# Left keys' values of four heads in one 64x32-tile pass behind a score burst, and g_q*g_k as a per-partition scale in the copy of transposed queries

## The chip, the cores and the metric

The kernel runs on one core of a Trainium2 chip. The metric is the device time in microseconds of one execution; where a kernel was run several times, the median is given.

## The reference

Two parts follow each other. Attention with normalised queries and keys, 8 batches, 12 heads, 448 positions, head dimension 64:

```
q_n = q / sqrt(mean(q*q) + 1e-6) * g_q          # the same for k with g_k
scores = q_n @ k_n.T / sqrt(64)
attn = softmax(scores)
x = attn @ v                                     # heads side by side: 3584 x 768
```

and a multiplicative feed-forward part on the 3584 x 768 result:

```
h = ((x @ w1) * (x @ w2)) @ w3                   # 768 -> 1024, 1024 -> 1024
out = h @ w_out                                  # 3584 x 768, float32
```

## The kernel before

**Quads and units.** Four heads of one batch are a "quad"; there are 24, three per batch. A quad's 448 keys are three full blocks of 128 (`NF` = 3) and 64 left keys (`REST`). Left keys of heads 0 and 1 lie in partitions 0 to 63 of the fourth value block, those of heads 2 and 3 in partitions 64 to 127; the other half of that block is zero or belongs to the other pair. The scores are made transposed, keys on partitions, in seven "units" a quad: `qk_exp` (L464) takes two PSUM banks, runs eight matmuls on 64x32 tiles (two heads on the two row tiles, four column tiles), and ScalarE takes the exponential of both banks into `P`, or into `Pr` for the left keys (L478). Units are issued in "bursts" of three (`G`).

**Sums and values.** `pv_set` (L494) is called three times a quad. Kind 0 multiplies `P` by ones: the softmax sums, of which ScalarE makes the reciprocal `r` as exp(-ln(sum)) (L507, L509). Kinds 1 and 2 multiply by the lower and the upper 32 columns of each head's values. Each is a set of four passes (`j` = 0 to 3) of four matmuls on 128x32 tiles, one head to a column tile, in one bank; the fourth pass is for the left keys. VectorE multiplies the bank by `r` into `xT` (L517). The places of the three kinds are set by `KIND`: steps of one unit behind the quad's last burst.

**Feed-forward fillers.** `ffn1_a` makes `a_sb` = x @ w1, `ffn1_b` multiplies x @ w2 by it into `abT` (L596), `ffn2` multiplies `abT` by `w34s` = w3 @ w_out into `o_sb`; all three go through `narrow` (L530), 24 or 32 matmuls on 128x32 tiles in one bank. These wait in a list, and the loop at the end puts some of them behind each unit's step (`UNITS`, `V_COST`), so that TensorE has work while ScalarE makes exponentials. At the start, while weights are still landing, w3 is transposed (`w3_transpose`, L546) and multiplied by w_out (`w34_unit`, L558).

**Preparation.** For each quad and each pair of heads: squares on ScalarE (L342), their sums on VectorE (L351), the factor `alpha` on ScalarE, and three multiplications on VectorE (`prep_scale`): queries by alpha (L383), that by g_q*g_k from `g_b`, which holds the product in every partition (L390), and keys by alpha (L397). For the first five quads (`N_PE_T`) TensorE transposes queries and keys (`prep_pe_transpose`, L432), with one VectorE copy of both from one bank (two banks and two copies in quad 0); for the rest a DMA on SP's queue does (L409).

**Who sets the order.** The program is written out by hand: a planner keeps an estimated clock of TensorE, ScalarE and VectorE (`clk`), the time at which each of the eight banks becomes free (`free`; `take` gives the earliest) and the landing times of the loads (`LAND`). From these it decides at the time of writing where each preparation and each eviction stands in its engine's stream (`drain`, `evac`; `SLACK`, `PACE`, `URGE`, `LATE` are its margins). `evac` chooses between ScalarE and VectorE where a string such as `A_EV = 'AD'` allows both. Nothing of this is decided while the kernel runs: each engine works through its stream in order and waits for semaphores. Weights and values are loaded on POOL's queue in the order of `LOADS`, queries and keys of later quads on SP's.

Of the kernel before, what the change touches and what calls it, by code (L numbers as in the profile page):

```python
# [18 lines left out]
def kernel(  # L19
# [32 lines left out]
    O_BUFS = 3  # L52
    F_BUFS = 9
    G = 3
    KIND = (2, 3, 6)
    N_PE_T = 5
    N_SQ_ACT = 24
    A_EV = 'AD'
    O_EV = 'AD'
    W_EV = 'DA'  # L60
    BIAS = 0.6
    SLACK = (0.5, 0.2)
    EXP_SLACK = 1.05
    WARM = 16
    WARM_GAP = 0.3
    PACE = 1.1
    SLACK_0 = (2.4, 0.6)
    URGE = 0.3
    AHEAD = 0.0
    LAG = 7  # L70
    UNITS = 1.45
    V_COST = 0.75
    V_AHEAD = 11
    LOAD_AT = -23
    LATE = 6
    T0 = 8.0
    LOADS = ['w1', 'q1', 'w0', 'o0', 'w2', 'v0', 'q2', 'w3', 'w4', 'w5', 'w6', 'v1', 'w7', 'o1', 'v2', 'x0', 'x1', 'v3']
    GATE = None
    GATE_T = {1: 13.0, 2: 11.0}
    AVAIL = 15.0  # L80
    LAND = {'g': 5.6, 'q1': 10.4, 'w0': 11.6, 'w1': 12.9, 'o0': 18.4, 'w2': 20.1, 'v0': 23.8, 'q2': 27.0, 'w3': 28.6, 'w4': 30.3, 'w5': 32.0, 'w6': 33.6, 'v1': 37.2, 'w7': 38.5, 'o1': 45.2, 'v2': 48.1, 'x0': 56.0, 'v3': 61.3, 'x1': 64.5, 'q3': 23.9, 'q4': 37.0, 'q5': 52.5, 'q6': 69.6}

    const = ctx.enter_context(tc.tile_pool(name="const", bufs=1))
    load_pool = ctx.enter_context(tc.tile_pool(name="load", bufs=3))
# [114 lines left out]

    ENG = {"A": "ACT", "D": "DVE"}  # L200

    def copy(e, out, in_):
        if e == "ACT":
            nc.scalar.copy(out=out, in_=in_)  # L204
        else:
            nc.vector.tensor_copy(out=out, in_=in_)  # L206

    def copy_out(z, out, in_, engs, n, bf=False):
        c = {"A": 0.19 + 0.81e-3 * n, "D": 0.12 + (0.55e-3 if bf else 1.06e-3) * n}
        return evac(  # L210
            z, clk["PE"], [ENG[x] for x in engs], [c[x] for x in engs],
            lambda e: copy(e, out, in_),
        )

    w1s = const.tile([128, CM, DFF], BF, name="w1s")
# [3 lines left out]
    w3s = big_pool.tile([128, CF, DFF], BF, tag="big", name="w3s")  # L219
    w3T = big_pool.tile([128, CF, DFF], BF, tag="big", name="w3T")  # L220
    g_row = const.tile([1, 2, D], FP, name="g_row")
    gp_row = const.tile([1, D], BF, name="gp_row")
    ones_row = const.tile([1, NP], BF, name="ones_row")
    g_b = const.tile([NP, D], BF, name="g_b")
    ident = const.tile([128, 128], BF, name="ident")
    ones = const.tile([NP, 3, HALF], BF, name="ones")
    warm_t = const.tile([128, 512], BF, name="warm_t")
# [65 lines left out]
    def load_w12(z):  # L293
        dst, src = ((w1s, moe_w1), (w2s, moe_w2))[z]
        for h in range(HQ):
            for half in range(2):
                nc.gpsimd.dma_start(
                    out=dst[h * HALF : (h + 1) * HALF, half::2, :],
                    in_=src.rearrange(
                        "(s h a d) f -> h a d s f", s=NQB, h=HQ, a=2, d=HALF  # L300
                    )[h, half],
                )
# [68 lines left out]
    def prep_scale(i, pr, part):  # L371
        s = st[i]
        hs = slice(2 * pr, 2 * pr + 2)
        alpha = s["alpha"]
        if "qkT" not in s:
            s["qkT"] = qkT_pool.tile([128, 2, 2, J * NP], BF, tag="qkT", name="qkT")
        if ("qks", pr) not in s:
            live["qks"] += 1
            s["qks", pr] = prep_pool.tile([NP, 2, J, 2, D], BF, tag="qks", name="qks")
        n = rows_of(i, 0)  # L380
        if part == 0:
            s["qtmp"] = prep_pool.tile([NP, J, 2, D], BF, tag="qtmp", name="qtmp")
            nc.vector.tensor_tensor(  # L383
                out=s["qtmp"][0:n].transpose([0, 2, 1, 3]),
                in0=s["q"][0:n, hs],
                in1=alpha[0:n, 0, hs].unsqueeze(3).broadcast_to([n, 2, J, D]),
                op=MULT,
            )
        elif part == 1:
            nc.vector.tensor_tensor(  # L390
                out=s["qks", pr][0:n, 0],
                in0=s["qtmp"][0:n],
                in1=g_b[0:n].unsqueeze(1).unsqueeze(1).broadcast_to([n, J, 2, D]),
                op=MULT,
            )
        else:
            nc.vector.tensor_tensor(  # L397
                out=s["qks", pr][:, 1].transpose([0, 2, 1, 3]),
                in0=s["k"][:, hs],
                in1=alpha[:, 1, hs].unsqueeze(3).broadcast_to([NP, 2, J, D]),  # L400
                op=MULT,
            )
# [11 lines left out]
    def prep_pe_transpose(i, pr):  # L414
# [1 line left out]
        issued.add(("t", i, pr))  # L416
        live["qks"] -= 1
        qks = s.pop(("qks", pr))
        both = i == 0
        if not both:  # L420
            ps, z = take(1)
            ps = ps.bitcast(BF)[:, 0 : 2 * S].rearrange("p (t s) -> p t s", t=2)
        for t in (1, 0) if i == 0 else (0, 1):
            if both:
                ps, z = take(1)
                dst = ps.bitcast(BF)[:, 0:S]
            else:
                dst = ps[:, t]
            w = NP0 if rows_of(i, t) < NP else NP
            for j in range(J):  # L430
                n = min(w, S - j * w)
                nc.tensor.transpose(  # L432
                    dst[:, j * w : j * w + n], qks[0:n, t, j], ident[0:n, 0:n]
                )
            run("PE", 0.25)
            if both:
                s["t_at", pr] = copy_out(
                    z, s["qkT"][:, pr, t, 0:S], dst, "DA"[t] if pr == 0 else "D", S, True
                )
        if not both:  # L440
            s["t_at", pr] = copy_out(z, s["qkT"][:, pr, :, 0:S], ps, "D", 2 * S, True)

# [34 lines left out]
        ))  # L479


    def pv_set(i, kind):
        s = st[i]
        b, m = divmod(i, NQB)
        flush_exps()
        ps, z = take(1)
        ps = ps[:, 0:S]
        for j in range(J):
            for h in range(HQ):
                if kind:  # L490
                    w = s["v"][:, h, j, (kind - 1) * HALF : kind * HALF]
                else:
                    w = ones[:, 0 if j < NF else 1 + h // 2, :]
                nc.tensor.matmul(  # L494
                    out=ps[h * HALF : (h + 1) * HALF, :],
                    lhsT=w,
                    rhs=s["P"][:, h, j, :] if j < NF else s["Pr"][:, h % 2, :],
                    start=(j == 0),
                    stop=(j == J - 1),
                    tile_position=(0, h * HALF),  # L500
                )
        run("PE", 0.77)
        if kind == 0:
            s["r"] = att_pool.tile([128, S], FP, tag="r", name="r")
            evac(
                z, clk["PE"], ["ACT"], [0.55],
                lambda e: nc.scalar.activation(out=s["r"], in_=ps, func=AF.Ln),  # L507
            )
            nc.scalar.activation(out=s["r"], in_=s["r"], func=AF.Exp, scale=-1.0)  # L509
            s["r_at"] = run("ACT", 0.57)  # L510
            kinds_done[0] = 3 * i + 1
            return
        if b not in xT:
            xT[b] = x_pool.tile([128, CM, S], BF, tag="xT", name="xT")
        evac(
            z, max(clk["PE"], s["r_at"]), ["DVE"], [0.64],
            lambda e: nc.vector.tensor_tensor(  # L517
                out=xT[b][:, 2 * m + kind - 1, :], in0=ps, in1=s["r"], op=MULT
            ),
        )  # L520
        kinds_done[0] = 3 * i + kind + 1
        if kind == 2:
            s.clear()
            if m == NQB - 1:
                push_ffn(b)


    def narrow(ps, n, lhsT, rhs, start, stop):
# [148 lines left out]
    def push_prep(n, avail, pairs=(0, 1)):  # L677
# [20 lines left out]
        for pr in pairs:  # L698
            x = al
            for part, c in enumerate((0.72, 0.44, 0.72)):  # L700
                x = add(
                    "sc", pr, "DVE", c,
                    lambda pr=pr, part=part: prep_scale(n, pr, part), x,
# [31 lines left out]
    with tc.manual_schedule():  # L735
# [34 lines left out]

        for t in range(2):
            prep_sq(0, 0, t)
        for t in range(2):
            prep_red(0, 0, t)
        try_load(7.0)
# [1 line left out]
        prep_alpha(0, 0, 2)  # L777
        prep_scale(0, 0, 2)
        prep_scale(0, 0, 0)
        nc.vector.scalar_tensor_tensor(  # L780
            out=gp_row, in0=g_row[:, 0], scalar=8.0, in1=g_row[:, 1], op0=MULT, op1=MULT
        )
        g_ps, z = take(1)
        g_ps = g_ps[:, 0:D]
        free[z] = 0.0
        nc.tensor.matmul(out=g_ps, lhsT=ones_row, rhs=gp_row, start=True, stop=True)
        nc.vector.tensor_copy(out=g_b, in_=g_ps)
        prep_scale(0, 0, 1)
        for e in clk:
            clk[e] = T0  # L790
        prep_pe_transpose(0, 0)
# [65 lines left out]
        def burst(m):  # L857
            flush_exps()
            for _ in range(m):
                qk_exp(units[0])  # L860

        while w34q or not fillers or clk["PE"] < LAND["x1"]:
            res = choices()
# [41 lines left out]
        todo = {}  # L905
        for x in range(kinds_done[0], 3 * NQ):
            i, kind = divmod(x, 3)
            last = NU * (i + 1) - 1
            at = step(last) + KIND[kind] if last >= t0 else t0 + x - kinds_done[0]
            todo.setdefault(at, []).append((i, kind))  # L910
# [1 line left out]
            t  # L912
            for t in sorted(todo)
            for i, kind in todo[t]
            if kind == 2 and i % NQB == NQB - 1
        ]
        room = lambda t: UNITS - V_COST * len(todo.get(t, []))
        for t in range(t0, max(todo) + 1):
            if next_load[0] < NQ and t >= next_load[0] * NU + LOAD_AT:
                try_load()  # L920
# [9 lines left out]
                try_v()  # L930
            pe_ops()
            last = min([p for p in pushes if p >= t] or [t])
            every = sum(room(z) for z in range(t, last + 1))
            fill(int(old * room(t) / every + 0.5))
            pe_ops()
        flush_exps()
        fill(len(fillers))
# [28 lines left out]
```

## Time and profile before

| | us |
|---|---|
| median of 5 runs | 376.64 (375.56 to 377.44) |
| the profiled execution | 375.56 |
| its span, first to last instruction | 373.7 |
| around the span | 1.86 |
| mean granted TensorE clock | 0.988 |

The page gives for each engine the time in which it had an instruction under way, and its share of the span. PE are matmuls, PEld the weight loads that overlap them, DVE is VectorE, ACT is ScalarE, POOL is GpSimd, SP the queue that issues DMAs. Matmuls are pipelined and their ends are modelled, so the length of a stretch of matmuls is read from its start to the start of what follows it, not from the durations. A group's line gives the source line, the engine, the operation, the tile written and those read, and the idle time before it with what ended it.

### The profile page before, as it was taken

Reading aid. Unit: us, or ns where it says so; the run is one execution under the profiler, and the core shown is the slowest. Engines: PE = TensorE matmul, PEld = TensorE weight load, DVE = VectorE, ACT = ScalarE, POOL = GpSimd, SP = SyncE. Lnnn points to the kernel's source line nnn. Section 1 sums busy time; section 2 is a strip of 40 time slices with the busy share of each in tenths; the row PEclk is TensorE's granted clock in tenths of the full one; section 3 lists DMA queues with packets and bytes.
Section 4 is the critical chain, followed back from the end, with each engine's and each line's share of the span. In section 5 each row is a group of like instructions: output and inputs, shape, how many; then the busy total and the mean of one; then the engine's idle time right before and its main releaser. Section 6 shows DMA issues by size and latency. Waiting matters only on the chain.

```text
span 373.7 us, 17079 instructions
## 1 busy us (share of the span) xinstructions
PE 361.9 (97%) x7657; PEld 195.0 (52%) x7659; DVE 244.1 (65%) x433; ACT 275.9 (74%) x464; POOL 80.2 (21%) x138
## 2 busy tenths in 40 slices
PE   6789999999999999999999999999999999999994
PEld 2445555455555555555555555555555555555562
DVE  4799988788787755877586758775786663222211
ACT  4667767888987798798887898888878976752231
POOL 7445444520222022202220201220220200000000
PEclk9699999999999999999999999999999999999998
DMA  7999999985999987998799599959892852014015
GB/s 189 212 217 237 220 225 229 179 161 121 192 206 171 160 134 156 229 162 107 151 194 189 99 182 182 197 137 156 182 188 43 112 148 56 2 29 105 2 25 149
DMA packets 91305, 56.43 MB, mean 151 GB/s; under 512 B 56928, under 2 KB 84640, under 8 KB 91232
## 3 DMA queue, kind: packets, MB, share of 16 engines
q1 hardware_dynamic: 68080, 40.61, 53.2%
q0 software_dynamic: 22560, 14.16, 26.7%
q8 instruction: 60, 0.98, 1.1%
q10 hardware_dynamic: 592, 0.56, 0.5%
q14 instruction: 13, 0.11, 0.1%
HBM read 46.66 MB, written 11.01 MB: 154 GB/s over the span
## 4 chain that ended last, share of the span: by engine, by line
PE 91%; DVE 3%; DMA 2%; POOL 1%; issue 1%; ACT 1%; POOLq 0%
PE banks_ps L530 59%; PE banks_ps L494 16%; PE banks_ps L464 10%; PE banks_ps L558 5%; DMA w3s<-in_moe_w_dram 2%; PE banks_ps L432 1%; PE banks_ps L546 1%; DVE ssq L351 1%; DVE qks L397 1%; ACT P L478 0%; DVE qkT L206 0%; POOL k_sb L255 0%; DVE w3T L206 0%; DVE w34s L206 0%; POOL q_sb L255 0%
## 5 line engine op out<-in xcount | busy, mean ns | idle before, releaser
L478 ACT ACTIVATE P<-banks_ps 128x896 bf16<-128x896 f32 x144 | 124.2, 924 | 10.5 <-PE banks_ps L464 10.3
L287 POOL DMA_DIRECT2D v_sb<-in_v_dram x72 | 43.6, 618 | 191.6 <-PE banks_ps L494 170.5
L530 PE MATMUL banks_ps<-xT,w1s 128*32 128x448 bf16 x1536 | 83.5, 353 | 0.0
L530 PE MATMUL banks_ps<-xT,w2s 128*32 128x448 bf16 x1536 | 83.1, 353 | 0.0
L530 PE MATMUL banks_ps<-w34s,abT 128*32 128x384 bf16 (+2 forms) x1792 | 78.5, 326 | 0.0
L596 DVE TENSOR_TENSOR abT<-banks_ps,a_sb 128x448 bf16<-128x448 f32 x64 | 40.0, 624 | 41.4 <-PE banks_ps L530 35.7
L351 DVE TENSOR_REDUCE ssq<-sq 128x8 f32<-128x512 f32 (+1 forms) x96 | 62.0, 679 | 6.6 <-ACT sq L342 6.0
L530 PEld LDWEIGHTS <-abT 128*32 128x32 bf16 x1792 | 48.0, 97 | 26.7
L517 DVE TENSOR_TENSOR xT<-banks_ps,r 128x448 bf16<-128x448 f32 x48 | 29.8, 624 | 45.5 <-PE banks_ps L494 44.8
L530 PEld LDWEIGHTS <-w2s 128*32 128x32 bf16 x1536 | 40.7, 97 | 32.4 <-issue 1.5
L530 PEld LDWEIGHTS <-w1s 128*32 128x32 bf16 x1536 | 40.5, 97 | 31.9 <-issue 1.9
L204 ACT CAST a_sb<-banks_ps 128x448 bf16<-128x448 f32 x54 | 28.9, 536 | 32.8 <-PE banks_ps L530 32.3
L464 PE MATMUL banks_ps<-qkT 64*32 64x448 bf16 x1344 | 43.3, 355 | 0.8 <-DVE qkT L206 0.8
L494 PE MATMUL banks_ps<-P,v_sb 128*32 128x448 bf16 x576 | 36.0, 355 | 0.0
L383 DVE TENSOR_TENSOR qtmp<-q_sb,alpha 128x512 bf16<-128x512 f32 (+1 forms) x48 | 32.9, 686 | 2.8 <-ACT alpha L367 2.3
L204 ACT COPY o_sb<-banks_ps 128x384 f32<-128x384 f32 x38 | 18.2, 480 | 21.3 <-PE banks_ps L530 20.3
L397 DVE TENSOR_TENSOR qks<-k_sb,alpha 128x512 bf16<-128x512 f32 x48 | 32.8, 683 | 0.6 <-ACT alpha L367 0.6
L342 ACT ACTIVATE sq<-k_sb 128x512 f32<-128x512 f32 x48 | 30.6, 638 | 2.7 <-DMA k_sb<-in_k_dram 2.7
L342 ACT ACTIVATE sq<-q_sb 128x512 f32<-128x512 f32 (+1 forms) x48 | 30.5, 635 | 0.7 <-DMA q_sb<-in_q_dram 0.7
L494 PEld LDWEIGHTS <-v_sb 128*32 128x32 bf16 x768 | 16.7, 96 | 23.8 <-issue 14.9
L464 PEld LDWEIGHTS <-qkT 64*32 64x32 bf16 x1344 | 14.6, 91 | 24.2 <-issue 19.6
L478 ACT ACTIVATE Pr<-banks_ps 128x896 bf16<-128x896 f32 x24 | 22.2, 926 | 3.8 <-PE banks_ps L464 3.8
(52 smaller groups left out, 268.9 us busy)
## 6 DMA issues: line engine op xcount, KB each, us to landing
out_dram<-o_sb SPq DMA_DIRECT2D x48, 192.0 KB, 3.4
q_sb<-in_q_dram SPq DMA_DIRECT2D x21, 256.0 KB, 4.5
k_sb<-in_k_dram SPq DMA_DIRECT2D x21, 256.0 KB, 5.6
q_sb<-in_q_dram SPq DMA_DIRECT2D x21, 192.0 KB, 5.1
k_sb<-in_k_dram SPq DMA_DIRECT2D x21, 192.0 KB, 5.5
v_sb<-in_v_dram POOLq DMA_DIRECT2D x24, 96.0 KB, 4.8
w3s<-in_moe_w_dram POOLq DMA_DIRECT2D x8, 256.0 KB, 9.9
w_outs<-in_moe_w_out_dram POOLq DMA_DIRECT2D x4, 384.0 KB, 10.1
```

The lines of the kernel that those rows point to most:

```text
L204: nc.scalar.copy(out=out, in_=in_)
L287: nc.gpsimd.dma_start(out=dst.rearrange("p h j d -> p h (j d)"), in_=part.rearrange("p h j d -> p h (j d)"),)
L342: nc.scalar.activation(out=s["sq", pr][0:n, t], in_=(s["q"], s["k"])[t][0:n, 2 * pr : 2 * pr + 2], func=AF.Square,)
L351: nc.vector.tensor_reduce(out=s["ssq"][0:n, t, 2 * pr : 2 * pr + 2, :], in_=s["sq", pr][0:n, t], axis=AX, op=ADD,)
L383: nc.vector.tensor_tensor(out=s["qtmp"][0:n].transpose([0, 2, 1, 3]), in0=s["q"][0:n, hs], in1=alpha[0:n, 0, hs].unsqueeze(3).broadcast_to ...
L397: nc.vector.tensor_tensor(out=s["qks", pr][:, 1].transpose([0, 2, 1, 3]), in0=s["k"][:, hs], in1=alpha[:, 1, hs].unsqueeze(3).broadcast_to ...
L464: nc.tensor.matmul(out=sc[c0 : c0 + 32, u, 0:S], lhsT=qkT[u * D : (u + 1) * D, pr, 1, k0 : k0 + 32], rhs=qkT[u * D : (u + 1) * D, pr, 0, 0:S],
L478: lambda: nc.scalar.activation(out=dst, in_=sc[:, :, 0:S], func=AF.Exp),
L494: nc.tensor.matmul(out=ps[h * HALF : (h + 1) * HALF, :], lhsT=w, rhs=s["P"][:, h, j, :] if j < NF else s["Pr"][:, h % 2, :], start=(j == 0 ...
L517: lambda e: nc.vector.tensor_tensor(out=xT[b][:, 2 * m + kind - 1, :], in0=ps, in1=s["r"], op=MULT),
L530: nc.tensor.matmul(out=ps[32 * h : 32 * h + 32, 0:n], lhsT=lhsT[:, 32 * h : 32 * h + 32], rhs=rhs, start=start, stop=stop, tile_position=( ...
L596: lambda e: nc.vector.tensor_tensor(out=abT[bp][:, fi, odd * S : (odd + 1) * S], in0=ps[:, 0:S], in1=a_sb, op=MULT,),
```

## The change

The fourth pass of both value sets is replaced by one pass. `values` takes two banks at once, runs eight matmuls on 64x32 tiles for the left keys (two row tiles for the two pairs of heads, four column tiles), which begin the accumulation in both banks, and then the three full blocks of each bank on 128x32 tiles. Kinds 1 and 2 become one call, which `KIND` places at the step after the sums' one, where a burst is issued first. In the second bank the heads stand in the order 2, 3, 0, 1, since each tile of the array serves one product; so its multiplication by `r` is made in two pieces of 64 partitions, and the rows of w1 and w2 are loaded in the matching order.

In the first five quads the queries are no longer multiplied by g_q*g_k on VectorE. The product is made once as a column, `g_col`, and is the per-partition scale of the copy that brings the transposed queries from PSUM; queries and keys have a bank and a copy each, and ScalarE or VectorE may make it. The other quads keep L390.

With it come other margins of the planner, other landing times, one exchange in the order of loads, and a reserve of one filler (`HOLD`).

```diff
-    KIND = (2, 3, 6)
+    KIND = (2, 3, 4)
+    Q_EV = 'AD'
+    K_EV = 'DA'
-    SLACK = (0.5, 0.2)
+    SLACK = (0.1, 0.0)
-    PACE = 1.1
-    SLACK_0 = (2.4, 0.6)
-    URGE = 0.3
-    AHEAD = 0.0
+    PACE = 1.4
+    SLACK_0 = (2.4, 0.4)
+    URGE = 0.6
+    AHEAD = 0.6
-    UNITS = 1.45
-    V_COST = 0.75
-    V_AHEAD = 11
-    LOAD_AT = -23
-    LATE = 6
+    UNITS = 1.4
+    V_COST = 0.5
+    V_AHEAD = 9
+    HOLD = 1
+    X_PAIR = False
+    LOAD_AT = -29
+    LATE = 4
-    LOADS = [... 'w6', 'v1', 'w7', 'o1', ...]
+    LOADS = [... 'w6', 'w7', 'v1', 'o1', ...]
...
+            else:
+                nc.scalar.activation(out=out, in_=in_, func=AF.Copy, scale=by)
...
+            nc.vector.tensor_scalar(out=out, in0=in_, scalar1=by, scalar2=None, op0=MULT)
...
+                p0 = (h + 2 * half) % HQ * HALF
-                    out=dst[h * HALF : (h + 1) * HALF, half::2, :],
+                    out=dst[p0 : p0 + HALF, half::2, :],
...
-        if part == 0:
+        if part == 0 and i < N_PE_T:
+            nc.vector.tensor_tensor(
+                out=s["qks", pr][0:n, 0].transpose([0, 2, 1, 3]),
+                in0=s["q"][0:n, hs],
+                in1=alpha[0:n, 0, hs].unsqueeze(3).broadcast_to([n, 2, J, D]),
+                op=MULT,
+            )
+        elif part == 0:
...
+        for t in (1, 0) if i == 0 else (0, 1):
             ps, z = take(1)
-            ps = ps.bitcast(BF)[:, 0 : 2 * S].rearrange("p (t s) -> p t s", t=2)
+            ps = ps.bitcast(BF)[:, 0:S]
...
+            s["t_at", pr] = copy_out(
+                z, s["qkT"][:, pr, t, 0:S], ps, (Q_EV, K_EV)[t], S, True,
+                None if t else g_col,
+            )
...
+    def values(i):
...
+        two = [take(1) for _ in range(2)]
+        for c in range(HQ):
+            for r in range(2):
+                h = 2 * r + c % 2
+                up = int(c // 2 != r)
+                nc.tensor.matmul(
+                    out=two[up][0][c * HALF : (c + 1) * HALF, 0:S],
+                    lhsT=s["v"][r * REST : (r + 1) * REST, h, NF, up * HALF : (up + 1) * HALF],
+                    rhs=s["Pr"][r * REST : (r + 1) * REST, h % 2, :],
+                    start=True,
+                    stop=False,
+                    tile_position=(r * REST, c * HALF),
+                )
+        for up, (ps, z) in enumerate(two):
+            for j in range(NF):
+                for c in range(HQ):
+                    h = (c + 2 * up) % HQ
+                    nc.tensor.matmul(
+                        out=ps[c * HALF : (c + 1) * HALF, 0:S],
+                        lhsT=s["v"][:, h, j, up * HALF : (up + 1) * HALF],
+                        rhs=s["P"][:, h, j, :],
+                        start=False,
+                        stop=(j == NF - 1),
+                        tile_position=(0, c * HALF),
+                    )
+            def scale(e, ps=ps, up=up):
+                x = xT[b][:, 2 * m + up, :]
+                for p0, p1 in ((0, 64), (64, 128)) if up else ((0, 128),):
+                    r0 = (p0 + 64 * up) % 128
+                    nc.vector.tensor_tensor(
+                        out=x[p0:p1], in0=ps[p0:p1, 0:S], in1=s["r"][r0 : r0 + p1 - p0], op=MULT
+                    )
+            evac(z, max(clk["PE"], s["r_at"]), ["DVE"], [(0.64, 1.24)[up]], scale)
...
+                if part == 1 and n < N_PE_T:
+                    continue
...
-        prep_scale(0, 0, 1)
...
+            if kind == 2:
+                continue
...
-            fill(int(old * room(t) / every + 0.5))
+            keep = HOLD if t < max(pushes) else 0
+            fill(int(max(0, old - keep) * room(t) / every + 0.5))
```

## The prediction

> **What bounds the kernel now.** I read the page's busy shares first, then a table of three stretches, then the chain of waits, and last the order of time around one burst.
>
> The page's first part and its chain:
>
> ```profile
> PE 361.9 (97%) x7657; PEld 195.0 (52%) x7659; DVE 244.1 (65%) x433; ACT 275.9 (74%) x464; POOL 80.2 (21%) x138
> ...
> PE 91%; DVE 3%; DMA 2%; POOL 1%; issue 1%; ACT 1%; POOLq 0%
> ```
>
> The busy time of each engine by stretch (columns: PE, PEld, DVE, ACT, POOL, granted clock, DMA share, GB/s):
>
> ```profile
> 0.00:31.00 31.00, 24.33 (x225) 12.04 (x235) 22.83 (x52) 18.23 (x35) 16.77 (x33) 0.89 1.05 209
> 31.00:65.00 34.00, 33.65 (x448) 18.57 (x436) 29.75 (x56) 25.64 (x43) 16.85 (x29) 1.00 1.19 228
> 65.00:335.00 270.00, 270.00 (x6232) 144.04 (x6228) 184.57 (x316) 222.98 (x369) 46.56 (x77) 1.00 0.82 146
> ```
>
> From 31 us on TensorE has no hole; all its idle time lies ahead of that. In the list of waits from 70 us on TensorE's matmuls do not occur at all. So after 31 us the time is TensorE's work, one in-order stream: a pass taken out of it is gained in full, and a wait put into it is lost in full. Other engines cost nothing unless they make it wait.
>
> The stream around one burst of score matmuls, in order of time (start, duration, engine, line):
>
> ```profile
> 202.25 1.31 PE L530 MATMUL banks_ps<-xT,w1s 128*32 128x448 bf16 x24
> ...
> 203.05 0.58 ACT L509 ACTIVATE r<-r 128x448 f32<-128x448 f32 x1
> 203.49 0.32 PEld L464 LDWEIGHTS <-qkT 64*32 64x32 bf16 x24 [0.37 <-issue]
> 203.49 0.76 PE L464 MATMUL banks_ps<-qkT 64*32 64x448 bf16 x24
> 203.61 0.53 ACT L204 CAST a_sb<-banks_ps 128x448 bf16<-128x448 f32 x1
> ...
> 204.18 0.75 PE L494 MATMUL banks_ps<-P,v_sb 128*32 128x448 bf16 x12
> 204.76 0.36 PE L494 MATMUL banks_ps<-Pr,v_sb 128*32 128x448 bf16 x4
> 204.76 1.05 PEld L530 LDWEIGHTS <-w2s 128*32 128x32 bf16 x24
> 204.95 1.31 PE L530 MATMUL banks_ps<-xT,w2s 128*32 128x448 bf16 x24
> 205.25 0.62 DVE L517 TENSOR_TENSOR xT<-banks_ps,r 128x448 bf16<-128x448 f32 x1 [2.24 <-PE banks_ps L494]
> ```
>
> From start to start: 16 value matmuls take 204.95 - 204.18 = 0.77, so a pass of four (128x32 tiles side by side) takes **0.19 us**. 24 score matmuls take 0.69: three passes of eight (64x32 tiles), 0.57, and 0.12 to leave that tiling. Entering it costs about 0.10 (24 filler matmuls last 1.14 elsewhere, here 1.24). Evictions follow late: ScalarE begins 0.12 after the burst starts, that is 0.22 after the last filler ended; VectorE begins 0.30 after its matmuls ended (205.25 against 204.95).
>
> [...] The new pass sends both row tiles into both banks, but into different quadrants. The trace does not show that: each row tile of a score unit has a bank of its own.
>
> **The change part by part.** Times are summed against the profiled execution, 375.56 us (span 373.7, 1.86 around it). That is the lowest of the five; the median is 1.08 higher, and I add the sum to the median.
>
> *Passes.* Per quad the values took two sets of four passes, the fourth for the left keys (64 rows of use in 128). Now there are one pass of 64x32 tiles and two sets of three: 7 in place of 8. The sums' set stays. 24 quads x 0.19 = **-4.6**, all on TensorE's path.
>
> *Tiling changes.* In the built order the pass stands directly behind a score burst in quads 3 to 22, so no change is added there. In quads 0 to 2 and 23 it stands alone: 4 x 0.10 = **+0.4**.
>
> *A new wait for a bank.* A burst takes six of eight banks, the values formerly one more. Now they take two at their start, so all eight. I followed each bank through the built order. Before, the shortest TensorE work between the last write of a bank and its next use is about 1.3 us in the steady stretch. After, in 19 quads one of the two banks is that of the filler directly ahead of the burst, used again 0.57 us after the burst's start (three passes; leaving the tiling comes later). In quad 3 the burst's own third unit meets it, at 0.38. When is it free? Start of the eviction + its duration + the way back to TensorE, 0.05 (a transposed copy at 18.18 lasting 0.38 released a matmul at 18.61). The filler's eviction is on ScalarE with a_sb in 5 quads: 0.12 + 0.53 + 0.05 = 0.70, wait 0.13; on ScalarE with o_sb in 6: 0.48 in place of 0.53, wait 0.08; on VectorE in 8: it begins 0.17 to 0.20 after the burst's start, 0.17 + 0.62 + 0.05 = 0.84, wait 0.27; quad 3: 0.84 - 0.38 = 0.46. Sum 0.65 + 0.48 + 2.16 + 0.46 = **+3.8**. Behind the waiting matmul stands the whole stream. Low end 20 x 0.08 = 1.6; high end, with one more VectorE operation (0.68) ahead of the eviction in the 9 quads of VectorE, 3.8 + 6.1 = 9.9. The order shows its predecessors nearly always done, so I take 3.8.
>
> *Evictions of the values.* The second half is multiplied in two pieces of 64 partitions, which I take at a full 0.62 each: 24 x 0.62 = 15 us more on VectorE. The cover is its idle time: (184.6 + 13)/270 = 73% after 65 us. The first filler behind the values comes 1.14 later, VectorE is then about 0.1 behind, and no bank hangs on it for two fillers: **0**; without that cover up to +0.1 a quad, +2. No gain is possible.
>
> *Queries.* In the five quads transposed on TensorE the multiplication by g_q*g_k (L390) goes: 10 x 0.42 = 4.2 us of VectorE; eight copies of 0.62 become sixteen of about 0.39, nine of all twenty on ScalarE (0.53). The scale rides in the copy: nearest row the copy itself, L204 0.53 or L206 0.39[...]. This lies in the first 70 us, VectorE 74 to 88% busy. After 10 us TensorE waited there on VectorE for about 2.4 us in all, and otherwise on the landing of w3. The first burst of scores now stands ahead of the first transposes of w3, and quad 1's first burst ahead of those of the fourth block of w3, which waited for their load until 28.95; one burst, 0.67, comes to lie in idle time. **-0.6**, between -2 and +1.5 (copies that ScalarE makes behind exponentials).
>
> *Order and loads.* Slacks, lateness and queue order of w7 and v1 move instructions, add no work and no DMA on any queue. On SP the transposing DMAs are issued at least 6.6 us of TensorE work ahead of use (7.3 before; their landing took 4.7, at most 6.6), nearly all over 8. POOL's loads of w7 and v1 change places, one behind the other. **0**, up to +1 if a transpose is late; a gain has no wait to come from.
>
> Sum: -4.6 + 0.4 + 3.8 - 0.6 = **-1.0**: 376.64 - 1.0 = 375.6 us (the profiled one 374.6). About 0.5% is what a measurement of this kernel can tell from no change, 1.9 us.
>
> **The rivals.** *The waits are short and the front gains more*: every eviction is as quick as o_sb's, 20 x 0.08 = 1.6, and the front gives 1.2: -4.6 + 0.4 + 1.6 - 1.2 = -3.8, 372.8. For it: planned order, ScalarE free at the burst in the trace. Against: 0.62 of VectorE can't fit into 0.57.
>
> *VectorE is busy when the last filler ends* (slower): in the nine quads that it evicts, a scale or a reduction of 0.68 holds it, half to all of it: +3.1 to +6.1, middle 4.6: -1.0 + 4.6 = +3.6, 380.2. It turns the result to slower from (1.0 + 1.9)/9 = 0.32 a quad. For: VectorE gets 15 us more work. Against: 27% of idle time and an order in which the eviction comes next.
>
> *The eight matmuls don't run as one pass*: row tiles that meet in a bank go one after the other, two passes, 24 x 0.19 = +4.6; the packing then saves nothing: 380.2 too. [...]
>
> **How the numbers follow.** The sum's case, within 1.9 us: 0.44, its own range 374.8 to 378.5. The short waits: 0.32. VectorE busy: 0.15; no single pass: 0.09. Faster 0.32, same 0.44, slower 0.24. The range 372.3 to 380.2 leaves out about one in ten at each end.
>
> **What would show it.** In the profile after: a group of 192 left-key matmuls on 64x32 tiles, eight in about 0.19 us, right behind the scores; 576 of P with v_sb as before; waits of TensorE, or a longer start-to-start time at that group, near 0.1 where ScalarE evicted the last filler, near 0.3 where VectorE did. Wrong: no lengthening there (then 372.8), waits above 0.6, eight matmuls taking 0.38, or TensorE idle after 31 us on qkT or on xT.

## The result, and the profile after

| | before | after |
|---|---|---|
| median, us | 376.55 (47 runs, 375.44 to 379.15) | 378.12 (26 runs, 375.57 to 385.55) |
| ratio to before | 1 | **1.0031** (95% interval 1.0017 to 1.0045) |
| the profiled execution, us | 375.56, span 373.7 | 377.09, span 375.3 |

The change makes the kernel slower by 0.3%. The medians of all runs differ by 1.6 us; the ratio, which leaves out two slow runs of the changed kernel (383.38 and 385.55), makes it 1.2 us. The forecast, a gain of 1.0 us, would be a ratio of 0.997 and lies below the interval. The single runs of the changed kernel also lie further apart.

The page of the changed kernel, its first and third part and its chain. The line of q8 counts the packets that carry instructions (packets, MB, share of the 16 DMA engines). The page before has the same 60 packets, at 1.1%, and the prediction did not use them:

```profile
PE 362.1 (96%) x7657; PEld 196.9 (52%) x7660; DVE 245.0 (65%) x433; ACT 285.2 (76%) x487; POOL 80.2 (21%) x138
...
q8 instruction: 60, 0.98, 1.2%
...
PE 94%; DVE 2%; ACT 2%; issue 1%; DVEq 0%
```

The same three stretches as before (columns: PE, PEld, DVE, ACT, POOL, granted clock, DMA share, GB/s):

```profile
0.00:31.00 31.00, 23.95 (x239) 11.91 (x243) 20.70 (x49) 19.36 (x38) 16.50 (x32) 0.89 1.05 204
31.00:65.00 34.00, 33.01 (x412) 17.96 (x413) 28.06 (x51) 26.43 (x46) 17.16 (x29) 1.00 1.19 226
65.00:335.00 270.00, 269.49 (x6216) 145.90 (x6208) 188.22 (x323) 228.34 (x384) 46.58 (x77) 1.00 0.84 146
```

TensorE now shows holes after 65 us, 0.5 us in all; before it showed none. More is hidden in the modelled ends of matmuls, so I measured every stretch of equal matmuls from its start to the start of the next and took off what such a stretch costs undisturbed (0.19 a pass, 0.1625 a pass of `ffn2`, whose 32 matmuls then take 1.30, 0.11 a change of tiling). From 65 us on the excess is 0.04 us before and **4.47 us** after. Some 4.1 us of it is of two kinds.

The first is the predicted wait for a bank. The order of time around a burst, evicted by ScalarE with a_sb:

```profile
207.22 0.76 PE L473 MATMUL banks_ps<-qkT 64*32 64x448 bf16 x24
207.34 0.53 ACT L209 CAST a_sb<-banks_ps 128x448 bf16<-128x448 f32 x1
...
207.80 0.51 PE L532 MATMUL banks_ps<-Pr,v_sb 64*32 64x448 bf16 x8
207.93 0.10 PEld L532 LDWEIGHTS <-v_sb 64*32 64x32 bf16 x6 [0.22 <-issue]
...
208.24 1.32 PE L545 MATMUL banks_ps<-P,v_sb 128*32 128x448 bf16 x24
```

The eviction ends at 207.87; the first of the eight matmuls, in the free bank, starts at 207.80, the other seven follow 0.13 later than without a wait (208.24 - 207.80 = 0.44, where the pass and the change of tiling need 0.31, as at 156.11). L545's 24 matmuls are six passes. Over the quads that wait, the sum is **3.41 us**: 0.08 each behind o_sb on ScalarE, 0.12 to 0.14 behind a_sb, 0.22 to 0.23 behind VectorE, 0.42 in quad 3.

The second kind was not predicted. The order of time around a filler at 190.56:

```profile
190.54 1.25 SPq L427 DMA_TRANSPOSE qkT<-qks  x1
190.56 0.93 PE L572 MATMUL banks_ps<-xT,w2s 128*32 128x448 bf16 x15
...
191.69 0.73 PE L572 MATMUL banks_ps<-xT,w2s 128*32 128x448 bf16 x9 [0.20 <-issue]
191.69 0.28 PEld L572 LDWEIGHTS <-w2s 128*32 128x32 bf16 x8 [0.64 <-issue]
```

In the middle of 24 equal matmuls, whose data and bank are ready, TensorE stands still for 0.38 us, and even its weight loads stop. "issue" says that it waited for nothing the profile shows. A second such hole, of 0.33 us, stands at 286.6. Numbered from TensorE's first, the instruction after such a hole has an index of 256 x n + 190 to 194, in every profile that has one. The q8 line agrees with the 256: TensorE's 15,331 instructions (matmuls, weight loads and a few others) are 59.9 blocks of 256, and there are 60 packets, each of 16 KB in the trace.

The start of each packet stands in the trace's DMA records (no view prints it). About one packet starts for each block, near the start of the block before it. For the hole above, the block before began at 185.4; the packet started at 189.03, took 1.3 us, and the block ran from 191.69, 2.7 us after the packet's start. So, as the traces read, **a block is fetched while the block before it runs** (about 5.5 us), and a packet that came late left TensorE idle, here for 0.38 us.

Where little else uses the DMA engines (from 310 to 369 us their share is 0.20 in the changed kernel) a packet mostly started 0.2 to 0.6 us ahead of the first instruction of the block before its own, some 6 us early. In the steady stretch, where the DMA engines are busy for 0.84 of the time, it started later, by the means below. In the 15 profiles of kernels without extra TensorE instructions, and 660 blocks from about 90 us on, 18 show such a hole, of 0.2 us or more. In all 18 the packet had started only 2.5 to 3.1 us ahead of where the block then began; of the 610 blocks with more than 3.1 us not one has it (leaving out waits for banks and for `abT` that fall there). The other 32 have a short lead and a smaller hole or none. One of them is in the profile of the kernel before, 0.16 us inside the burst of scores at 123.93, where the busy times hide it. The mean start of a packet, counted from the start of the block before (90 to 305 us), is 0.97 us before and 1.34 after; beyond 2 us lie 5 and 11.

### The profile page after: what moved, and what is told of

It reads as the page before. It is cut to its first block, busy times and chain, and to the rows that moved or that the text cites. A ratio compares the mean times of both kernels' runs of the same rounds, so it can differ in the third digit from the quotient of the medians.

```text
span 375.3 us, 17063 instructions
## 1 busy us (share of the span) xinstructions
PE 362.1 (96%) x7657; PEld 196.9 (52%) x7660; DVE 245.0 (65%) x433; ACT 285.2 (76%) x487; POOL 80.2 (21%) x138
## 4 chain that ended last, share of the span: by engine, by line
PE 94%; DVE 2%; ACT 2%; issue 1%; DVEq 0%
PE banks_ps L572 59%; PE banks_ps L473 10%; PE banks_ps L545 8%; PE banks_ps L600 5%; PE banks_ps L504 5%; PE banks_ps L532 2%; PE banks_ps L714 2%; PE banks_ps L443 2%; ACT P L487 1%; PE banks_ps L588 1%; ACT sq L353 1%; DVE qks L415 1%; DVE qks L393 1%; DVE ssq L362 0%; ACT lnv L375 0%
## 5 line engine op out<-in xcount | busy, mean ns | idle before, releaser
L559 DVE TENSOR_TENSOR xT<-banks_ps,r 64x448 bf16<-64x448 f32 (+1 forms) x72 | 44.8, 622 | 41.4 <-PE banks_ps L545 40.2
L572 PEld LDWEIGHTS <-abT 128*32 128x32 bf16 x1792 | 49.6, 97 | 26.0 <-issue 2.6
L209 ACT CAST a_sb<-banks_ps 128x448 bf16<-128x448 f32 x56 | 29.9, 534 | 26.4 <-PE banks_ps L572 25.4
L473 PE MATMUL banks_ps<-qkT 64*32 64x448 bf16 x1344 | 44.1, 357 | 1.5 <-ACT qkT L211 0.7
L209 ACT COPY o_sb<-banks_ps 128x384 f32<-128x384 f32 x51 | 24.3, 477 | 23.7 <-PE banks_ps L572 22.1
L401 DVE TENSOR_TENSOR qtmp<-q_sb,alpha 128x512 bf16<-128x512 f32 x38 | 26.2, 688 | 11.1 <-ACT alpha L378 10.2
L545 PE MATMUL banks_ps<-P,v_sb 128*32 128x448 bf16 x576 | 31.7, 354 | 0.0
L600 PE MATMUL banks_ps<-w_outs,w3T 128*128 128x384 bf16 x128 | 22.5, 327 | 0.0
```

The source lines that it names most:

```text
L473: nc.tensor.matmul(out=sc[c0 : c0 + 32, u, 0:S], lhsT=qkT[u * D : (u + 1) * D, pr, 1, k0 : k0 + 32], rhs=qkT[u * D : (u + 1) * D, pr, 0, 0:S],
L545: nc.tensor.matmul(out=ps[c * HALF : (c + 1) * HALF, 0:S], lhsT=s["v"][:, h, j, up * HALF : (up + 1) * HALF], rhs=s["P"][:, h, j, :], star ...
L559: nc.vector.tensor_tensor(out=x[p0:p1], in0=ps[p0:p1, 0:S], in1=s["r"][r0 : r0 + p1 - p0], op=MULT)
L572: nc.tensor.matmul(out=ps[32 * h : 32 * h + 32, 0:n], lhsT=lhsT[:, 32 * h : 32 * h + 32], rhs=rhs, start=start, stop=stop, tile_position=( ...
L600: nc.tensor.matmul(out=ps[:, 0:NH], lhsT=w3T[:, gc, fc * 128 : (fc + 1) * 128], rhs=w_outs[:, gc, nh * NH : (nh + 1) * NH], start=(gc == 0 ...
```

## The experiments

Medians of 6 to 22 runs, beside runs of the kernel before, whose median was 376.6 to 376.8 each time. "Delay" is the mean just described.

| kernel | median, us | ratio (interval) | delay, us |
|---|---|---|---|
| gcol_late | 378.85 | 1.0036 (1.0013 to 1.0059) | 1.41 |
| short_evict | 377.07 | 0.9994 (0.9972 to 1.0015) | 1.62 |
| unpacked | 382.62 | 1.0134 (1.0087 to 1.0182) | 1.30 |
| before_early | 376.69 | 0.9998 (0.9980 to 1.0017) | 1.01 |
| after_copy | 376.32 | 0.9980 (0.9966 to 0.9994) | 0.83 |
| before_copy | 377.45 | 1.0014 (0.9998 to 1.0030) | 0.69 |
| after_phase | 378.61 | 1.0046 (1.0028 to 1.0064) | 1.21 |
| after_margins | 381.19 | 1.0103 (1.0059 to 1.0148) | 1.22 |
| after_split | 378.27 | 1.0047 (1.0028 to 1.0066) | 1.27 |
| late_split | 378.34 | 1.0043 (1.0022 to 1.0063) | 1.47 |
| before_split | 376.23 | 0.9992 (0.9977 to 1.0007) | 0.83 |
| late_copy | 376.53 | 1.0001 (0.9984 to 1.0018) | 0.92 |
| short_copy | 373.63 | 0.9913 (0.9897 to 0.9930) | 0.89 |
| late_p46 | 379.05 | 1.0078 (1.0042 to 1.0113) | 1.55 |
| late_halves | 379.42 | 1.0094 (1.0061 to 1.0127) | 1.01 |

**The start: gcol_late and before_early.** In the changed kernel VectorE's copy into `g_col` waits for a matmul that stands behind 16 idle-time matmuls, and the first reductions wait behind the copy:

```profile
7.54 0.18 PE L832 MATMUL banks_ps<-gp_row,ones_row 1*128 1x64 bf16 x1
7.76 0.16 DVE L835 COPY g_col<-banks_ps 128x1 f32<-128x1 f32 x1 [2.32 <-PE banks_ps L832]
7.84 1.27 DVE L362 TENSOR_REDUCE ssq<-sq 112x8 f32<-112x512 f32 x2
```

Before, those reductions ran at 4.86 and 6.96. gcol_late moves the copy behind them:

```diff
-        nc.vector.tensor_copy(out=g_col, in_=g_ps[:, 0:1])
...
+        nc.vector.tensor_copy(out=g_col, in_=g_ps[:, 0:1])
         nc.vector.tensor_copy(out=g_b, in_=g_ps[:, 64 : 64 + D])
```

> The changed kernel with one instruction moved: the copy that makes g_col stands behind the two first reductions and the two first scales on VectorE, where before stood its g_b copy. Theory (start chain): in the changed kernel the first reduction began at 7.84 us because the g_col copy ahead of it waited for a matmul behind the sixteen warming matmuls (7.50); before, the first reduction began at 4.86 and the second at 6.96. The first transposes then come at about 9.7 in place of 11.20, the third block of w3 is transposed at about 29.0 in place of 29.61, and the kernel is 0.6 to 1.5 us faster than the changed one, 0 to 1 us slower than before. Rival (the start doesn't matter, the loads of w3 or ScalarE's copies set the time at 30 us): the first transposes come earlier, but the first use of w1s stays at 63.5 us and the time at 378.1.

Its first reduction:

```profile
5.21 0.67 DVE L362 TENSOR_REDUCE ssq<-sq 112x8 f32<-112x512 f32 x1
```

TensorE's first `ffn1_a` came at 61.69 us in place of 63.53. But the median is no lower, and one execution does not show a lead. Up to that matmul the changed kernel, short_evict, after_copy and short_copy are the same program, and their profiles have it at 63.53, 62.04, 63.93 and 63.21; before and before_copy, also the same program so far, have it at 62.56 and 63.49. The profile of gcol_late also has 0.22, 1.19 and 0.38 us of holes at the start of blocks, more than the changed kernel's. before_early does the reverse with the kernel before: the block of `gp_row`, its matmul and `g_b` stands ahead of the first reductions.

> The kernel before with one block moved: the product g_q*g_k, its matmul and the g_b copy stand ahead of the first two reductions, where the changed kernel has them. Theory (start chain): the first reduction waits until 7.8 us, the first transposes come about 1 us later than 10.25 and the kernel is 0.5 to 1.2 us slower than before, about 377.4. Rival (the start has slack in it, since the loads of w3 come later): no change, 376.5.

No difference. Its first reductions came at 6.86 in place of 4.86, and its first transposes no later than before (9.49 against 10.25): the kernel before has slack there.

**The waits for banks: short_evict.** The last filler ahead of a burst with values evicts a quarter of its columns; GpSimd sets the rest of its output to zero, so that part of the result is left out.

```diff
+                fill(n - 1)
+                cut[0] = True
+                fill(1)
+                cut[0] = False
...
+        w = S // 4 if cut[0] else S
-        at = copy_out(z, a_sb, ps[:, 0:S], A_EV, S)
+        at = copy_out(z, a_sb[:, 0:w], ps[:, 0:w], A_EV, S)
```

> The changed kernel, with a quarter of the columns evicted from the bank of the last filler ahead of each burst that has the values behind it (the other three quarters of that result are set to zero by GpSimd: that part of the feed-forward result is left out). Theory (the wait is for that bank): the eviction ends about 0.3 to 0.45 us earlier, the stretch from the start of such a burst to the first matmul of P with v_sb, now 0.94 to 1.3 us, becomes 0.88 in all twenty quads, and the time falls by 3 to 3.5 us against the changed kernel, to 374.6 to 375.1. Rival (the pass of eight matmuls itself runs slowly, because its row tiles meet in the banks): the stretches stay as they are and the time stays at 378.1.

The waits for banks are gone from its profile (at most 0.07), but the median falls by 1.05 us, not by 3.4. TensorE's list of waits from 70 us shows what came instead, a late transposing DMA and two holes at the start of blocks (columns: us in all, times, longest):

```profile
PE banks_ps L473 <- DMA qkT<-qks: 0.7, 1, 0.7
PE banks_ps L545 <- issue: 0.7, 1, 0.7
PE banks_ps L504 <- issue: 0.3, 1, 0.3
```

**The packing: unpacked.** The values as two sets of four passes again, all else as changed.

```diff
-            for j in range(NF):
+            for j in range(J):
...
-                        rhs=s["P"][:, h, j, :],
-                        start=False,
+                        rhs=s["P"][:, h, j, :] if j < NF else s["Pr"][:, h % 2, :],
+                        start=(j == 0),
```

> The changed kernel with the values as before: two sets of four passes on 128x32 tiles, one bank taken for each, both behind the burst; all else of the change is kept. Theory (net gain of the packing is the pass less the wait): each quad gains the waits, 3.4 us over twenty quads, and 0.4 us of tiling changes in four quads, and pays 24 passes of 0.19, 4.6 us: 0.8 us slower than the changed kernel, about 378.9; the second set starts without a wait. Rival (the packing is what made the change slower, through more than its bank wait): at least 1 us faster than the changed kernel, 377 or less.

4.5 us slower than the changed kernel, where the passes alone make 4.6 less 0.4 for tiling changes. Not a clean undoing: the planner's order shifts with it, and its profile has 9.7 us of excess, among it two waits of 0.9 for `abT` and one hole of 2.0 us at the start of a block. After that hole the granted clock (last but two of the columns) fell to 0.58 for 4.1 us:

```profile
124.30:126.80 2.50, 0.47 (x9) 0.03 (x2) 2.03 (x4) 0.37 (x1) 0.00 (x0) 1.00 1.24 95
126.80:130.90 4.10, 4.10 (x59) 1.43 (x59) 0.00 (x0) 2.22 (x4) 0.00 (x0) 0.58 1.00 234
```

**What makes the packets late: after_copy and before_copy.** The theory by now was that packets come late behind data, behind the transposing DMAs above all: in the steady stretch the transposes' packets of 256 bytes took 0.27 of the time of all 16 DMA engines. Both kernels put plain DMAs of the same bytes in their place and leave the transposition out.

```diff
-        nc.sync.dma_start_transpose(
-            out=s["qkT"][:, pr].rearrange("d t (j p) -> d (t j) p", p=NP),
+        nc.sync.dma_start(
+            out=s["qkT"][:, pr].rearrange("d t x -> d (t x)"),
```

> The changed kernel, with each of the 38 transposing DMAs (qkT<-qks) replaced by a plain DMA of as many bytes between the same two tiles: the scores of quads 5 to 23 are made from untransposed data, everything else and the order stay. Theory (TensorE's instructions come in blocks of 256, one 16 KB packet of the instruction queue each; a packet that starts less than about 2.9 us ahead of its first instruction leaves TensorE idle, and packets start late because data DMAs, the transposing ones most, fill the DMA engines: 0.27 of the time of all 16 in the steady stretch): no idle time of TensorE with 'issue' from 90 to 305 us at instruction 190 of a block (changed kernel: 0.4 and 0.3 us), packets start at most 2.5 us behind the start of the block before (changed kernel: up to 3.6), median 376.4 to 377.3 and a narrower spread than the changed kernel's. The waits for banks stay at 3.4 us. Rival (the packets are late for the loads and the stores, or the stalls aren't the packets'): stalls at the same index in the profile, the median within 0.5 us of the changed kernel's 378.1.

> The kernel before, with its 38 transposing DMAs replaced by plain ones in the same way (scores of quads 5 to 23 from untransposed data). Theory of late instruction packets: the kernel before has 0.16 us of such idle time in its profile, so it gains little: 375.4 to 376.3 (before 376.6), mostly from executions that lie above 377. With it the pair without transposing DMAs stands at a ratio near 1.001 to 1.003 or lower. Rival (transposes have nothing to do with it): 376.6 as before, and the pair's ratio stays 1.003 to 1.004.

As many bytes in fewer packets: the page's line of q1 (packets, MB, share of the engines) is for the changed kernel and then for after_copy

```profile
q1 hardware_dynamic: 68080, 40.61, 54.6%
```

```profile
q1 hardware_dynamic: 33424, 40.61, 40.4%
```

The changed kernel gains 1.8 us, its delay falls to 0.83, and its quartiles draw together (377.0 to 379.0 becomes 375.8 to 376.8). One hole stays, 0.57 us at 115.2, and the largest delay is 3.9, so packets come late without transposing DMAs too. The edit takes away two things at once: traffic ahead of the packets, and late landings of `qkT` itself. The profile of the changed kernel shows no wait for `qkT`, but five of the 13 profiles with transposing DMAs do (short_evict 0.7 us, unpacked 0.4, after_margins 2.3, late_p46 1.0, late_halves 0.4), all in the changed order. The holes at block starts are larger: in the ten profiles of that order with transposing DMAs they come to some 1.8 us a profile in the mean, against 0.5 for the waits on `qkT`, and in the three of the kernel before (before, before_early, before_split) to some 0.2, with no such wait.

The kernel before did not gain; it came out 0.8 slower (the interval just reaches 1), a miss. Its profile shows one hole, at instruction 191 of a block:

```profile
239.88 0.73 PE L530 MATMUL banks_ps<-xT,w2s 128*32 128x448 bf16 x9
...
241.25 0.94 PE L530 MATMUL banks_ps<-xT,w2s 128*32 128x448 bf16 x15 [0.64 <-issue]
```

It is as large as the median's loss (0.82 us of excess), but that is one execution, and its first `ffn1_a` came 0.9 late as well. What made the other executions slower is open. The mean delay alone, 0.69 here, does not tell the time.

**Place or block: after_phase and late_p46.** Extra matmuls in idle time at the start shift the blocks against the work.

```diff
-                out=ps, lhsT=warm_t[:, 0:128], rhs=warm_t, start=True, stop=True
+            for c in range(4):
+                    out=ps[:, c * 128 : (c + 1) * 128], lhsT=warm_t[:, 0:128],
+                    rhs=warm_t[:, c * 128 : (c + 1) * 128], start=True, stop=True
```

> The changed kernel with each of its 23 idle-time matmuls of 512 columns on the zero tile (16 at the start, 7 in the gaps until 29 us) cut into four of 128 columns: 69 matmuls and 69 weight loads, 138 instructions more on TensorE, all where it has nothing to do, so that the blocks of 256 instructions begin some 3 us earlier in the work. Theory of late packets: idle time with 'issue' stands again at instruction 190 of a block, therefore at other fillers than in the changed kernel (there at 191.7 and 286.6 us); the sum of such stalls may be smaller or larger, the median anywhere from 376.8 to 379.5. Rival (the stalls belong to the place in the work: a filler beside a transposing DMA or late data): the stalls stay at 191.7 and 286.6 us, at the same matmuls, now at another index of a block, and the median within 0.5 us of 378.1.

> gcol_late with each of the 23 idle-time matmuls of 512 columns cut into two of 256: 46 instructions more, all in idle time, so that the blocks of 256 begin about 1 us earlier in the work. Theory: stalls with 'issue' again at instruction 190 of a block, in other sizes than gcol_late's (0.22, 1.19, 0.38); median between 376 and 379.5, by the chance of the alignment. Rival (the place in the work decides): 378.5 to 379.2 with stalls at the same matmuls as gcol_late.

In after_phase the holes left 191.7 and 286.6 and stand at 117.7 (1.05 us, a wait for a bank of 0.2 in it), 233.9 (0.39) and 279.2 (0.65), each again at instruction 193 of a block. The last of them:

```profile
278.41 0.35 PE L572 MATMUL banks_ps<-xT,w1s 128*32 128x448 bf16 x1
...
279.23 0.92 PE L572 MATMUL banks_ps<-xT,w1s 128*32 128x448 bf16 x13 [0.47 <-issue]
```

In late_p46 (two pieces in place of four, on gcol_late) they stand at 114.8, 121.6, 129.7, 202.3 and 280.2, 2.2 us the largest. The block decides, not the place in the work. Neither alignment is a better one in the median.

**Spreading the traffic: after_split, late_split, before_split, late_halves, after_margins.** The keys' two loads of a quad three units behind the queries':

```diff
+            if keys and t >= keys_at[0]:
+                load_k(keys.pop())
...
-                try_load()
+                try_load(later=keys)
+                if keys:
+                    keys_at[0] = t + 3
```

> The changed kernel with the four loads of a later quad parted in the steady stretch: its two loads of queries where all four stood, its two of keys three units of work (about 5 us) later; same bytes, nothing else moved by hand. Theory (what makes an instruction packet late is a pile of data DMAs issued together): mean delay of a packet from 90 to 305 us falls from 1.34 us to 1.0 or less, none over 3.2 us, no 'issue' stalls in the profile, median 376.6 to 377.5. Rival (the amount of data decides, not how it is bunched, or the transposing DMAs alone): delay and stalls as in the changed kernel, median 377.7 to 378.6.

> The same parting of the loads, and the copy into g_col moved behind VectorE's first reductions and scales (as in gcol_late, which won 1.8 us at the start and lost them again in stalls). Theory of late packets: with the stalls gone the gain of the start is kept: 374.8 to 376.0, faster than both kernels. Rival: a gain at the start is always given back (something later sets the time): within 0.6 us of after_split.

> The kernel before with the same parting of the loads. Theory: its packets were late by 0.97 us in the mean and only one stall of 0.16 us was in its profile; 375.9 to 376.7, spread no wider. Rival (another place of the loads meets the packets just as well or worse, it is the chance of the alignment): up to 378, with a stall at instruction 192 of a block.

A miss for the changed kernel: holes of 0.50 and 1.56 us, beside transposing DMAs again, and no gain. In before_split there is no hole left, the largest delay is 2.1, but the gain of 0.4 us lies within the interval. late_halves cuts each transposing DMA in two instead:

```diff
+                if part == 1:
+                    add("t0", pr, "SP", 0.0, lambda pr=pr: prep_dma_transpose(n, pr, 0), x)
```

> gcol_late with each transposing DMA cut in two: the queries' half is issued as soon as they are multiplied by g_q*g_k, the keys' half as before; 38 more DMAs on SP's queue, same bytes. Theory (a pile of data issued at once makes a packet late): mean delay of a packet under 1.2 us (gcol_late 1.41), stalls under 0.8 us, median 376.0 to 377.5. Rival (the transposes' amount decides, or SP's queue, which holds each transpose some 1.2 us, becomes late itself): 378.5 to 380, with TensorE waiting for qkT.

Its profiled execution is quick (375.98) and its delay low, with one hole of 0.2 and a wait of 0.4 for `qkT`, yet its median is 379.4. One profile does not show what the others do, and this stays open. after_margins:

```diff
-    SLACK = (0.1, 0.0)
+    SLACK = (0.5, 0.2)
-    LOAD_AT = -29
-    LATE = 4
+    LOAD_AT = -23
+    LATE = 6
...
```

> The changed kernel with the margins of the kernel before for the steady stretch: SLACK (0.5, 0.2), SLACK_0's second 0.6, PACE 1.1, URGE 0.3, AHEAD 0, V_AHEAD 11, LOAD_AT -23, LATE 6. Theory that the changed margins (queries and keys loaded 29 units ahead in place of 23, values 9 in place of 11, preparation forced 4 units ahead in place of 6) make the instruction packets late: the mean delay of a packet falls from 1.3 us to that of the kernel before, 1.0, stalls of the 'issue' kind under 0.3 us, median 376.9 to 377.6. Rival (margins without effect, the packing alone makes the traffic collide, or chance of the alignment): 377.9 to 378.5 and a mean delay of 1.3.

A miss: the delay only falls to 1.22. Waits for banks rise to 0.56, and one burst of scores is held for its transposed data, whose DMA took 8.5 us to land (at most 6.6 in the kernel before, 7.8 in the changed one):

```profile
103.33 2.60 SPq L427 DMA_TRANSPOSE qkT<-qks  x1
...
111.86 0.57 PE L473 MATMUL banks_ps<-qkT 64*32 64x448 bf16 x16 [2.28 <-DMA qkT<-qks]
```

Four of the five profiles with such waits have one at this place, between 108 and 112 us.

**The terms of the sum without transposing DMAs: late_copy and short_copy**, which are gcol_late and short_evict with after_copy's edit.

> gcol_late (the copy into g_col behind VectorE's first reductions and scales) with plain DMAs for the transposing ones as in after_copy: scores of quads 5 to 23 from untransposed data. Theory (the start's delay is real and was masked by stalls): 374.5 to 375.5, 1 to 1.8 us below after_copy's 376.3. Rival (the start has slack behind it, so its delay costs nothing): 376.0 to 376.6.

> short_evict (the last filler ahead of each burst with values evicts a quarter of its columns, GpSimd sets the rest to zero, and g_col is copied early as in the changed kernel) with plain DMAs for the transposing ones; part of the feed-forward result and the scores of quads 5 to 23 are left wrong. Theory (waits for banks cost their 3.4 us in full): 372.6 to 373.4. Rival (a wait taken away turns up as another one, on exponentials or packets): 374.5 to 376.

short_copy is 2.7 us below after_copy: most of the 3.4 us of waits for banks. A burst in it, evicted by VectorE, where the changed kernel waits 0.22:

```profile
232.22 0.76 PE L473 MATMUL banks_ps<-qkT 64*32 64x448 bf16 x24
...
232.35 0.28 DVE L213 CAST a_sb<-banks_ps 128x112 bf16<-128x112 f32 x1 [0.86 <-PE banks_ps L572]
...
232.80 0.37 PE L532 MATMUL banks_ps<-Pr,v_sb 64*32 64x448 bf16 x8
...
233.10 1.32 PE L545 MATMUL banks_ps<-P,v_sb 128*32 128x448 bf16 x24
```

From L532 to L545 there are 0.30 us: eight matmuls in 0.19 and 0.11 to leave the tiling. late_copy is no faster than after_copy (376.53 against 376.32), though its profile is 1.1 us ahead at the first `ffn1_a`. So the place of the copy into `g_col` costs nothing that a median shows, and a lead of 1.1 us in one pair of executions is within what the same program shows from one execution to the next (62.04 to 63.93).

## Why the prediction was wrong, step by step

- **Passes, -4.6: right.** The eight matmuls ran as one pass of 0.19 (0.30 with the change of tiling, at 232.80 in short_copy) though both row tiles write into each bank, in different groups of 32 partitions. That they would, no trace of the kernel before had shown. The rival of two passes is out.
- **Wait for a bank, +3.8: right.** 3.41 us in the profile, 2.7 in medians; each class within 0.05 of its forecast. The rivals of short waits and of a busy VectorE are out.
- **Evictions of the values and scaled copies, 0: right.** Two pieces of 64 partitions cost 0.62 each, and TensorE waits for none of them. The scaled copies took 0.45 on VectorE and 0.63 on ScalarE, 0.06 and 0.1 above the plain copies' 0.39 and 0.53 that were put in for them.
- **Start, -0.6: not shown either way.** The profile has +1.0 at the first `ffn1_a`, but there the same program differs by 0.9 and 1.9 us between executions. What is seen is that the copy into `g_col`, priced at nothing, put VectorE's first reductions behind a matmul that ends at 7.7; moving it brought no gain in medians (gcol_late +0.7, late_copy +0.2 against their partners, within the noise).
- **Order and loads, 0, up to +1: the step that failed.** It priced only what the moved DMAs bring late to `qkT`, and took TensorE's list of waits, empty before, as proof that nothing else hangs on DMA traffic. But TensorE's own instructions came by DMA too (60 packets of 16 KB), and the profile of the kernel before already has a hole of 0.16 us at the start of a block. Taking the transposing DMAs out gives 1.8 us to the changed kernel and takes 0.8 from the one before: in medians a relative 2.6 us, by the ratios 2.4. The landing of `qkT` was also judged by the kernel before, at most 6.6 us; in the changed order it took up to 7.8, and in after_margins 8.5, with waits in five profiles.

Two readings of the kernel before were off. The prediction says that TensorE has no hole from 31 us on; its own table has 33.65 of 34.00 us busy from 31 to 65, and the hole at 123.93 lies in a stretch that shows as fully busy. Neither changes the sum.

Without transposing DMAs the pair stands at 376.32 - 377.45 = -1.1 us, where the sum said -1.0. That agreement is partly luck, since the loss of before_copy against before is unexplained; but 378.12 - 376.55 = +1.6 is that -1.1 with 2.7 put on by the transposing DMAs. That instruction packets carry most of this is what the profiles say, not a run that separates them from late `qkT`. What in the changed order piles up the traffic was not settled: neither the loads' bunching (after_split) nor the margins alone (after_margins) explain it. No version with the real transposes beat the kernel before beyond its interval.

## What to carry to other kernels

In this kernel, where TensorE runs thousands of small instructions almost without a hole, its instruction stream used the DMA engines beside the data (60 packets of 16 KB, 1.2% of their time). In a kernel like it, compare the packets of the page's instruction queue with the engine's instructions, and their starts with the starts of the blocks, before pricing a move of data DMAs at nothing. A stall "for issue" inside a run of equal matmuls, at the same index modulo 256, was its mark here. The pass saved by taking two banks at once was paid back in part by the last eviction: of 4.6 us, 3.4 came back as waits of 0.1 to 0.4. And before a lead in one profile is explained, compare it with profiles of kernels that are the same program up to that point; here these differed by up to 1.9 us.

## What the runs showed of the hardware that I had not expected

- Every hole of 0.2 us or more at the start of a block of 256 TensorE instructions, 18 in 15 profiles, had its packet of 16 KB started only 2.5 to 3.1 us ahead of it, although the packet itself took 0.9 to 1.6 us in the changed kernel; beside data DMAs its packets started up to 3.6 us after the block before had begun.
- After a hole of 2.0 us in unpacked the granted clock was 0.58 for 4.1 us; after a hole as long in late_p46 it stayed at 1.0 for the 3.3 us read.
- In one pass both row tiles of 64x32 matmuls wrote into the same two banks, in different groups of 32 partitions. Where no bank was waited for (156.11 in the changed kernel), the eight began within 0.02 us of each other and what follows them 0.31 us after the first; a pass of the score bursts and leaving the tiling took as long (0.19 and 0.12).
